# Strassen's scheme for the first product of the second MLP, last two batches

## The chip, the cores and the metric

The kernel runs on one core of a Trainium2 chip. The metric is the time on the device of one execution, in microseconds (us). The engines are named as in the profile: PE multiplies matrices (PEld is its loading of the stationary operand), DVE, ACT and POOL work on rows of 128 partitions, and SP issues the transfers (DMA).

## What is computed

Attention over 4 batches, 12 heads, 448 positions and head size 64, with normalised queries and keys, feeds two MLPs without a residual. Only the second one is changed.

```python
    x = attn_out.transpose(0, 2, 1, 3).reshape(B * S, H * D)      # 1792 x 768
    a = x @ w1; b = x @ w2; h = a * b @ w3; x = h @ w_out         # first MLP, 1024 wide
    h = x @ w_in                                                  # second MLP, 768 x 2048
    g = h * np.clip(h + 3.0, 0.0, 6.0) / 6.0
    return g @ w_out                                              # 2048 x 768
```

Inputs are float64 on the host and come as 64-bit words; the kernel converts them to float32 itself.

## The kernel before

Every product is made in float32 from halves: a value is split into a high part, rounded by ACT to the matmul's format, and a low part, the rest; `mm3` takes three matmuls for a product, high by high, high by low and low by high. A matmul has a stationary tile of 128 x 128 and 448 columns.

A scheduler sets the order of each engine's instructions, by the order in which the program issues them and by its own estimate of when each can run; `tc.issue_after` holds an instruction behind another one. Attention is first, with the product of w3 and w_out beside it, and the batches of the first MLP follow each other (`layer1`, `layer2`), the last one (batch 3) after the end of attention. Its weights `ws` are read back from DRAM, two halves of 768 columns in one transfer of 768 KB each, on SP's queue. In this time the weights of the second MLP begin to be read (`wr`, 768 KB of 64-bit words per tile of 128 x 768) and converted: `convert` takes two ACT and two DVE instructions per tile (L137, L138, L140, L143), and the results `wf`, 32 tiles, stay in SBUF to the end. `NA = 17` of them are made before the second MLP, the other 15 during its first batch.

The second MLP takes the batches in the order 3, 0, 1, 2, and in each 16 steps `m` of 128 hidden units. Step m has 18 matmuls for h (6 tiles of x, `mm3` each, into one bank), and 18 matmuls of the step before for the output (`l4_part`, six banks that collect over all m). Between them h becomes g: ACT makes the clipped part (L930), DVE multiplies by h (L931), ACT and DVE split the result (L934, L935). Each step splits its two weight tiles anew, ACT the high part (L851), POOL the low part (L852):

```python
    def split(q, tag, pool=None):
        t = (pool or lp).tile([P, 2, DM], F32R, tag=tag, bufs=2 if pool is None else 1, name=tag)
        nc.scalar.activation(t[:, 0, :], wf[q], AF.Copy)
        nc.gpsimd.tensor_sub(t[:, 1, :], wf[q], t[:, 0, :])
        return t
```

At the change of batch x is read from DRAM (`x2d`) and split by L826 and L827. Conversions of batch 3 stand in program order at the head of each step.

Of the kernel before, what the change touches and what calls it, by code (L numbers as in the profile page):

```python
# [47 lines left out]
def fused_kernel(ctx: ExitStack, tc: tile.TileContext, nat, qT, kT, vin, gq, gk,  # L48
# [8 lines left out]
    x2d = dpool.tile([B - 1, KD, P, S], F32, name="x2d")  # L57
    wpd = dpool.tile([KD * M1 // 6, P, 6, 2 * P], F32, name="wpd")
# [246 lines left out]
    def xsplit(i):  # L305
        d = L["pool"].tile([P, 2, S], F32R, tag="xhl", bufs=XB, name="xhl")
# [517 lines left out]
    def splitx2(n, src):
        d = x2p.tile([P, 2, S], F32R, tag="x2h", bufs=KD, name="x2h")
        nc.scalar.activation(d[:, 0, :], src, AF.Copy)  # L826
        nc.vector.tensor_sub(d[:, 1, :], src, d[:, 0, :])  # L827
        xh[n] = d

    L["x2"] = lambda n, ps: splitx2(n, ps[:, :S])  # L830

    def load_w(q):
        if q < 2 * M2:
            pool, tag, n = (wap, "wr", 2)
            if q >= NA + 2 and (q - NA) % 4 > 1:
                pool, tag, n = (lp, "wr", 1) if (q - NA) % 4 == 2 else (wap, "w0", 1)
            wr[q] = fetch(pool, (win, wo2)[q % 2][q // 2], DM, tag, bufs=n)

    def conv_w(q):
        r = wr.pop(q)  # L840
        wf[q] = wpools[-1].tile([P, DM], F32, name=f"wf{q}")
        if r.dtype == F32:
            nc.gpsimd.tensor_copy(wf[q], r)
        else:
            for _ in convert(wf[q].bitcast(I32), r):
                pass
        load_w(q + (2 if q < NA else 4))

    def split(q, tag, pool=None):
        t = (pool or lp).tile([P, 2, DM], F32R, tag=tag, bufs=2 if pool is None else 1, name=tag)  # L850
        nc.scalar.activation(t[:, 0, :], wf[q], AF.Copy)  # L851
        nc.gpsimd.tensor_sub(t[:, 1, :], wf[q], t[:, 0, :])  # L852
        return t

    load_w(0)
    load_w(1)
    step, q = 0, 0
    while not state["done"] or any(k >= now[0] for k in tasks):
# [3 lines left out]
        step += 1  # L862
# [75 lines left out]
    for e in (before, pend):  # L938
        for n in range(KD):
            with tc.issue_after(mm.ins) if mm else ExitStack():  # L940
                mm = l4_part(n, *e)
            if e is pend:
                out(n, t, acc)
# [47 lines left out]
```

## Time and profile before

| | |
|---|---|
| runs | 1225.72, 1224.61, 1220.15 us |
| median | 1224.61 us |
| profiled execution, first to last instruction | 1219.5 us |
| PE busy | 1160.4 us (95%), 5868 matmuls |
| DVE / ACT / POOL busy | 756.6 / 726.6 / 464.9 us |
| DMA | 203.73 MB, mean 167 GB/s |

The span is the time from the first to the last instruction of one execution that was profiled; the runs were timed apart and contain what lies around the span. Busy times are sums of the durations of an engine's instructions. In a window of the trace a matmul's duration overlaps that of the next, so PE's time per matmul is the window over its count and not the mean duration.

### The profile page before, as it was taken

The page shows a single profiled execution, that of the slowest core. Times are in us where ns is not written, and L with a number is a line of the kernel's source. Part 1 is how long each engine was busy: PE and PEld are TensorE (multiplying, and loading weights), DVE is VectorE, ACT ScalarE, POOL GpSimd, SP SyncE. Part 2 cuts the span into 40 slices and gives each one's busy share as a digit, 9 for nine tenths or more (in the row PEclk, how much of TensorE's full clock was granted, in tenths as well). Part 3 has the DMA queues.
Part 4 walks back from the last instruction along what each step waited for, and adds up shares of the span by engine and source line. Part 5 has one row for each costly group of instructions (what it writes and reads, how often), then busy time and mean ns, then how long its engine had stood idle before and what let it go on. Part 6 is the DMA issues. An engine that isn't in the chain of part 4 may idle for free.

```text
span 1219.5 us, 16961 instructions
## 1 busy us (share of the span) xinstructions
PE 1160.4 (95%) x5868; PEld 1020.5 (84%) x5868; DVE 756.6 (62%) x1474; ACT 726.6 (60%) x1401; POOL 464.9 (38%) x316
## 2 busy tenths in 40 slices
PE   3699998899999999999999999999999999999998
PEld 2457887777788999899999998999999999999997
DVE  6977888899976787677633447884333433343332
ACT  6888788899866767666634436664433443344332
POOL 3534224645522213212020005555455445544452
PEclk9799998999999999999999999999999999999999
DMA  7668565788987677666459985430200020001001
GB/s 277 209 220 239 191 188 196 251 284 293 334 265 254 222 224 249 228 240 197 148 187 360 355 304 207 156 101 23 91 1 1 4 88 1 1 1 46 1 1 46
DMA packets 64694, 203.73 MB, mean 167 GB/s; under 512 B 8544, under 2 KB 25440, under 8 KB 64608
## 3 DMA queue, kind: packets, MB, share of 16 engines
q1 hardware_dynamic: 64608, 202.65, 49.4%
q8 instruction: 46, 0.75, 0.3%
q14 instruction: 40, 0.33, 0.1%
HBM read 173.93 MB, written 28.68 MB: 166 GB/s over the span
## 4 chain that ended last, share of the span: by engine, by line
PE 75%; DVE 7%; ACT 5%; DMA 5%; issue 4%; POOL 3%; SPq 0%; ACTq 0%; POOLq 0%; DVEq 0%
PE bank L340 10%; PE acc L81 7%; PE acc L83 7%; PE acc L82 6%; PE h L81 6%; PE h L82 6%; PE h L83 6%; PE bank L345 5%; PE bank L592 4%; PE bank L81 3%; PE bank L82 3%; PE bank L83 3%; DVE PP L573 2%; PE bank L566 2%; PE bank L567 2%
## 5 line engine op out<-in xcount | busy, mean ns | idle before, releaser
L852 POOL TENSOR_TENSOR wis<-wf,wis 128x768 fp32r<-128x768 f32 x63 | 120.0, 1904 | 220.0 <-ACT wis L851 219.9
L340 PE MATMUL bank<-xhl,ws 128*128 128x448 f32 x768 | 184.9, 372 | 2.5 <-ACT bs L316 2.4
L931 DVE SCALAR_TENSOR_TENSOR u<-u,h 128x448 f32<-128x448 f32 x64 | 39.5, 618 | 210.6 <-ACT u L930 210.6
L340 PEld LDWEIGHTS bank<-xhl,ws 128*128 128x128 f32 x768 | 145.1, 191 | 16.5 <-ACT bs L316 3.1
L852 POOL TENSOR_TENSOR wos<-wf,wos 128x768 fp32r<-128x768 f32 x64 | 121.4, 1896 | 91.0 <-ACT wos L851 91.0
L585 ACT ACTIVATE PP<-PP,mx 112x448 f32<-112x448 f32 x192 | 127.2, 664 | 45.0 <-DVE mx L580 36.4
L573 DVE CUSTOM_DVE_ANT_0 PP<-bank,rb,rq 112x448 f32<-112x448 f32 x192 | 129.0, 675 | 34.8 <-PE bank L567 23.9
L83 PE MATMUL acc<-g,wos 128*128 128x448 f32 x384 | 141.3, 368 | 0.0
L82 PE MATMUL acc<-g,wos 128*128 128x448 f32 x384 | 141.3, 368 | 0.0
L81 PE MATMUL acc<-g,wos 128*128 128x448 f32 x384 | 140.0, 368 | 0.0
L81 PE MATMUL h<-x2h,wis 128*128 128x448 f32 x378 | 139.2, 368 | 0.5 <-DVE u L931 0.4
L82 PE MATMUL h<-x2h,wis 128*128 128x448 f32 x378 | 138.9, 367 | 0.0
L83 PE MATMUL h<-x2h,wis 128*128 128x448 f32 x378 | 137.4, 364 | 1.3 <-POOL wis L852 1.3
L930 ACT ACTIVATE u<-h,half 128x448 f32<-128x448 f32 x64 | 40.7, 636 | 156.0 <-PE h L83 156.0
L935 DVE TENSOR_TENSOR g<-u,g 128x448 fp32r<-128x448 f32 x64 | 105.2, 1645 | 37.5 <-ACT g L934 37.5
L851 ACT ACTIVATE wos<-wf 128x768 fp32r<-128x768 f32 x64 | 54.2, 847 | 85.9 <-PE acc L83 85.7
L601 ACT ACTIVATE xh<-bank 128x448 fp32r<-128x448 f32 (+1 forms) x156 | 83.0, 539 | 32.6 <-PE bank L592 29.4
L566 PE MATMUL bank<-K,Q 128*112 128x448 f32 x192 | 76.7, 400 | 25.6 <-DVE mx L573 13.1
L611 DVE TENSOR_TENSOR xl<-bank,xh 128x448 fp32r<-128x448 f32 x142 | 87.3, 616 | 21.9 <-ACT xh L601 20.6
L592 PE MATMUL bank<-ident,PP 112*128 112x112 f32 x672 | 94.4, 264 | 6.0 <-DVE xl L611 5.2
L592 PEld LDWEIGHTS bank<-ident,PP 112*128 112x128 f32 x672 | 77.7, 142 | 26.8 <-issue 6.8
L345 PE MATMUL bank<-xhl,ws 128*128 128x448 f32 x384 | 95.4, 367 | 0.0
(134 smaller groups left out, 2604.5 us busy)
## 6 DMA issues: line engine op xcount, KB each, us to landing
ws<-w12d SPq DMA_DIRECT2D x48, 768.0 KB
ws<-wpd SPq DMA_DIRECT2D x32, 768.0 KB
raw<-in_w_dram SPq DMA_DIRECT2D x32, 384.0 KB
w12d<-ws SPq DMA_DIRECT2D x16, 768.0 KB
wr<-in_wo_dram SPq DMA_DIRECT2D x16, 768.0 KB
qr<-in_qT_dram SPq DMA_DIRECT2D x24, 448.0 KB
kr<-in_kT_dram SPq DMA_DIRECT2D x24, 448.0 KB
nat<-in_nat_dram SPq DMA_DIRECT2D x23, 448.0 KB
```

Source lines behind the costliest of these rows:

```text
L81: nc.tensor.matmul(ps, lh, rh, start=first, stop=False)
L82: nc.tensor.matmul(ps, lh, rl, start=False, stop=False)
L83: return nc.tensor.matmul(ps, ll, rh, start=False, stop=last)
L340: nc.tensor.matmul(ps[:, :S], w[:, 0, ks], x[:, y, :], start=k == 0 and y == 0, stop=False)
L345: nc.tensor.matmul(ps[:, :S], w[:, 1, ks], L["xhl"][i][:, 0, :], start=False, stop=k == KD - 1)
L566: nc.tensor.matmul(ps[:CP, :S], qs, k1[:, j, :], start=True, stop=False)
L573: anchors[8 * i + s].append(nc.vector.tensor_tensor_reduce(out=T["PP", i][:, c, sl], in0=ps[:CP, :S], in1=T["rb", i][:, sl], op0=ALU.mult, ...
L585: anchors[8 * i + s].append(nc.scalar.activation(v, v, AF.Exp, bias=T["m", i][:, 8 + s : 9 + s], accum_out=T["sum", i][:, s : s + 1]))
L592: nc.tensor.transpose(ps[:, c * CP : c * CP + CP], src[:, c, kb * P : kb * P + P], ident[:CP, :CP])
L611: nc.vector.tensor_sub(lo, ps, hi)
L852: nc.gpsimd.tensor_sub(t[:, 1, :], wf[q], t[:, 0, :])
L935: nc.vector.tensor_sub(g[:, 1, :], u, g[:, 0, :])]
```

## The change

The second MLP is now made in three passes. Pass 0 is batch 3, pass 1 is batch 0, both with the same 18 and 18 matmuls per step. Pass 2 takes batches 1 and 2 together: for two steps of m (a pair j) and the two halves of the 768 inputs, the 2 x 2 block product of the weights with x of the two batches is made from seven products P1 to P7 of 9 matmuls each, in place of eight. The sums of weight blocks (S1 to S4) are made on DVE at each pair (L992), the sums of x (T1 to T4) once, on DVE; two banks, sA and sB, collect the products, ACT copies a bank (L1109), and DVE adds a copy to a bank (L1117). The output of batch 1 is made during the pass, that of batch 2 after it, from the stored `G`. Weights are split in halves of 384 columns (`wt`, seven tiles, six made ahead), by ACT and POOL in passes 0 and 1, and by ACT and DVE or POOL in turn in pass 2 (`halves`). The converted tiles don't stay: a ring of 11 tiles holds them, six more lie in tiles that pass 2 needs later for x, and each tile is written to DRAM (`wfd`) after use in its first pass and read again in the next two. Conversions are spread by `spend`, a budget in us per step. Lines move by one from the top (L83 is now L84, the transfers' L89 is L90, L140 is L141, L143 is L144), from L340 on by six.

```diff
+    wfd = dpool.tile([2 * M2, P, DM], F32, name="wfd")
...
+            if b == B - 1:
+                L["xm"].__exit__(None, None, None)
+                L["half"] = True
...
+    NWF, NWT, AHEAD2 = 11, 7, 6
+    BATCHES = {0: (B - 1,), 1: (0,), 2: (1, 2)}
...
+    for p in range(2):
+        for m in range(M2):
+            v = use("in", m)
+            items += [("I", p, m, v, h) for h in range(2)] + late
+            late = last_out(p, m) if m < M2 - 1 else []
+        late = last_out(p, M2 - 1)
+    items[1:3] = items[2:0:-1]
+    for j in range(M2 // 2):
+        v = (use("in", 2 * j), use("in", 2 * j + 1))
+        ls = late
+        if j:
+            ls = last_out(2, 2 * j - 2) + last_out(2, 2 * j - 1)
+        late = []
+        ls = [ls[: len(ls) // 2], ls[len(ls) // 2 :]]
+        for z in ("P1", "P2", "P6", 0, "P5", "P7", 1, "P3", "P4"):
+            items += ls[z] if z in (0, 1) else [(z, 2, j, v, z == "P4")]
+    for q in (M2 - 2, M2 - 1):
+        items += last_out(2, q)
+    for q in range(M2):
+        v = use("out", q)
+        items += [("M", 2, q, v, h) for h in range(2)]
...
+    def units():
+        for v, (kind, q) in enumerate(uses):
+            if v in extra:
+                while "left" not in xo:
+                    yield None
+                t = xtile(("11", "21", "T2")[(v - NWF) // 3], (v - NWF) % 3)
+                t = t.bitcast(F32).rearrange("p t s -> p (t s)")[:, :DM]
+            else:
+                z = ring.index(v) - NWF
+                while z >= 0 and ring[z] not in dropped:
+                    yield None
+                t = mp.tile([P, DM], F32, tag="wf", bufs=NWF, name="wf")
+            if v in fresh:
+                r = wr.pop(v)
+                if r.dtype == F32:
+                    nc.gpsimd.tensor_copy(t, r)
+                    yield 0.9
+                else:
+                    yield from convert(t.bitcast(I32), r)
+                load_raw()
+                yield 0.0
+            else:
+                dma(t, wfd[q + (M2 if kind == "out" else 0)])
+                yield 0.0
+            wf[v] = t
...
+    def drop(v):
+        kind, q = uses[v]
+        t = wf.pop(v)
+        dropped.add(v)
+        if v in fresh:
+            dma(wfd[q + (M2 if kind == "out" else 0)], t)
...
+    def halves(t, src, eng=None):
+        nc.scalar.activation(t[:, 0, :], src, AF.Copy)
+        if eng is None:
+            nsplit[0] += 1
+            eng = nc.vector if nsplit[0] % 2 else nc.gpsimd
+        eng.tensor_sub(t[:, 1, :], src, t[:, 0, :])
         return t
...
+    def xrest():
+        x = []
+        for k in range(KD // 2):
+            x.append(ptile())
+            dma(x[k], x2d[BATCHES[2][1], k + 3])
+        for k in range(KD // 2):
+            xo["22", k] = halves(xtile("22", k), x[k])
+            yield 1.2
+            d = ptile()
+            nc.vector.tensor_sub(d, xo["21", k][:, 0, :], xo["T2", k][:, 0, :])
+            nc.vector.tensor_sub(x[k], xo["21", k][:, 1, :], xo["T2", k][:, 1, :])
+            nc.vector.tensor_add(d, d, x[k])
+            xo["T4", k] = halves(xtile("T4", k), d)
+            yield 1.8
+
+    RIGHT = {"P1": "11", "P2": "21", "P6": "T2", "P5": "T1", "P7": "T3", "P3": "22", "P4": "T4"}
+    wt, sx = {}, {}
+
+    def prepare(i):
+        kind, p, j, v, h = items[i]
+        if kind[0] != "P":
+            upto(v)
+            t = mp.tile([P, 2, NH], F32R, tag="wt", bufs=NWT, name="wt")
+            wt[i] = halves(t, wf[v][:, h * NH : h * NH + NH], nc.gpsimd if p < 2 else None)
+            if h:
+                drop(v)
+            return
+        upto(v[1])
+        a11, a12 = wf[v[0]][:, :NH], wf[v[0]][:, NH:]
+        a21, a22 = wf[v[1]][:, :NH], wf[v[1]][:, NH:]
+
+        def temp(z, x, y, op):
+            sx[z] = xo["right"].tile([P, NH], F32, tag="sx", bufs=3, name="sx")
+            nc.vector.tensor_tensor(out=sx[z], in0=x, in1=y, op=op)
+            return sx[z]
+
+        if kind == "P6":
+            temp("S1", a21, a22, ALU.add)
+            temp("S2", sx["S1"], a11, ALU.subtract)
+        src = dict(P1=a11, P2=a12, P4=a22).get(kind)
+        if src is None:
+            if kind == "P7":
+                src = temp("S3", a11, a21, ALU.subtract)
+            elif kind == "P3":
+                src = temp("S4", a12, sx["S2"], ALU.subtract)
+            else:
+                src = sx["S2" if kind == "P6" else "S1"]
+        t = mp.tile([P, 2, NH], F32R, tag="wt", bufs=NWT, name="wt")
+        wt[i] = halves(t, src)
+        if h:
+            drop(v[0])
+            drop(v[1])
...
-        if step > 2 and q < NA and step % 3 == 0:
-            conv_w(q)
-            q += 1
-            if q == 1:
-                wnext = split(0, "w0", wap)
...
+        if L["cur"] < B * NU - 4 and (now[0] % 2 or "half" in L):
+            spend(1.5)
+        if "half" in L:
+            if "left" not in xo:
+                xo["left"] = d1.enter_context(tc.tile_pool(name="xl", bufs=1, side="left", **RW))
+            prep_to(ready[0] + 1 if ready[0] < AHEAD2 else 0)
...
+    def product(kind, i, ps, first):
+        w = wt.pop(i)
+        z = RIGHT[kind]
+        for k in range(KD // 2):
+            ks = slice(k * P, k * P + P)
+            x = xo[z, k]
+            for n, (a, c) in enumerate(((0, 0), (0, 1), (1, 0))):
+                mm = nc.tensor.matmul(ps[:, :S], w[:, a, ks], x[:, c, :], start=first and k == 0 and n == 0,
+                                      stop=k == KD // 2 - 1 and n == 2, skip_group_check=not first)
+        return mm
+
+    def strassen(i):
+        kind, p, j, _, _ = items[i]
+        if not swap:
+            swap.append((bank("s", "sA"), bank("s", "sB")))
+        a, c = swap[0]
+        own = c if kind in ("P2", "P5", "P3") else a
+        snap["mm"] = product(kind, i, own, kind in ("P1", "P2", "P5"))
+        r = own[:, :S]
+        if kind in ("P1", "P6", "P5"):
+            snap[kind] = utile()
+            nc.scalar.activation(snap[kind], r, AF.Copy)
+            return
+        if kind == "P4":
+            finish(p, j, 21, r)
+            swap[0] = (c, a)
+            return
+        s, z = {"P2": ("P1", 11), "P7": ("P5", 22), "P3": ("P6", 12)}[kind]
+        s = snap.pop(s)
+        nc.vector.tensor_add(s, r, s)
+        finish(p, j, z, s)
...
+    prep_to(AHEAD2)
+    xg = iter(())
+    for i, it in enumerate(items):
...
+        if i > 4:
+            with ExitStack() as es:
+                for z in done:
+                    es.enter_context(tc.issue_after(z.ins))
+                spend(1.0)
+        (plain if kind == "I" else strassen if kind[0] == "P" else layer4)(i)
```

SP's queue in the last batch of the first MLP, with `ws` the weights of the first MLP, `wr` the raw weights of the second, `wfd` the converted ones in DRAM. Before:

```order
L89 DMA ws<-w12d 128x1536 x2
L89 DMA wr<-in_win_dram 128x1536
L89 DMA ws<-w12d 128x1536 x2
L89 DMA wr<-in_wo_dram 128x1536
L89 DMA ws<-w12d 128x1536 x2
L89 DMA wr<-in_win_dram 128x1536
L89 DMA ws<-w12d 128x1536
L89 DMA wr<-in_wo_dram 128x1536
```

After the change:

```order
L90 DMA ws<-w12d 128x1536 x2
L90 DMA wr<-in_win_dram 128x1536
L90 DMA ws<-w12d 128x1536
L90 DMA wfd<-wf 128x768
L90 DMA ws<-w12d 128x1536
L90 DMA wr<-in_wo_dram 128x1536
L90 DMA ws<-w12d 128x1536
L90 DMA wfd<-wf 128x768
L90 DMA ws<-w12d 128x1536
L90 DMA wr<-in_win_dram 128x1536
L90 DMA ws<-w12d 128x1536
L90 DMA wfd<-wf 128x768
```

Each conversion is followed by a write of the converted tile, which stands between the loads of ws.

DVE's queue in the third and fourth step of batch 3 (L140/L141 and L143/L144 are the two DVE steps of a conversion, L931/L1048 the product with h, L935/L1056 the low half of g). Before:

```order
L931 SCALAR_TENSOR_TENSOR u<-u,h_8100 128x448
L935 TENSOR_TENSOR g<-u,g 128x448
L140 SCALAR_TENSOR_TENSOR wr<-wr 128x768
L143 SCALAR_TENSOR_TENSOR wf_8143<-wr 128x768
L931 SCALAR_TENSOR_TENSOR u<-u,h_8156 128x448
L935 TENSOR_TENSOR g<-u,g 128x448
L140 SCALAR_TENSOR_TENSOR wr<-wr 128x768
L143 SCALAR_TENSOR_TENSOR wf_8199<-wr 128x768
```

After the change:

```order
L1048 SCALAR_TENSOR_TENSOR u<-u,h_8093 128x448
L1056 TENSOR_TENSOR g<-u,g 128x448
L141 SCALAR_TENSOR_TENSOR wr<-wr 128x768 x2
L144 SCALAR_TENSOR_TENSOR wf<-wr 128x768 x2
L141 SCALAR_TENSOR_TENSOR wr<-wr 128x768
L144 SCALAR_TENSOR_TENSOR wf<-wr 128x768
L1048 SCALAR_TENSOR_TENSOR u<-u,h_8170 128x448
L1056 TENSOR_TENSOR g<-u,g 128x448
L141 SCALAR_TENSOR_TENSOR wr<-wr 128x768
L144 SCALAR_TENSOR_TENSOR wf<-wr 128x768
L141 SCALAR_TENSOR_TENSOR wr<-wr 128x768
```

Where one conversion stood between two products with h, two or three stand now.

DVE's queue at the change from batch 0 to the next (L827 and L928 make low halves, L969 and L970 combine parts of x, `wt` and `sx` are weights). Before:

```order
L931 SCALAR_TENSOR_TENSOR u<-u,h_9539 128x448
L935 TENSOR_TENSOR g<-u,g 128x448
L827 TENSOR_TENSOR x2h<-wr,x2h 128x448 x3
L827 TENSOR_TENSOR x2h<-w_8941,x2h 128x448 x3
L931 SCALAR_TENSOR_TENSOR u<-u,h_9588 128x448
L935 TENSOR_TENSOR g<-u,g 128x448
L931 SCALAR_TENSOR_TENSOR u<-u,h_9655 128x448
```

After the change:

```order
L1048 SCALAR_TENSOR_TENSOR u<-u,h_9920 128x448
L1056 TENSOR_TENSOR g<-u,g 128x448
L928 TENSOR_TENSOR wt<-wf,wt 128x384
L928 TENSOR_TENSOR xo<-xp,xo 128x448 x2
L969 TENSOR_TENSOR xp<-xo 128x448 x2
L928 TENSOR_TENSOR xo<-xp,xo 128x448
L970 TENSOR_TENSOR xp<-xp 128x448 x2
L969 TENSOR_TENSOR xp<-xo 128x448
L1048 SCALAR_TENSOR_TENSOR u<-u,h_9979 128x448
L928 TENSOR_TENSOR wt<-sx,wt 128x384
L970 TENSOR_TENSOR xp<-xp 128x448
L992 TENSOR_TENSOR sx<-wf,sx 128x384
```

Six subtractions of x stood behind the low half of g; now splits of weights and x, and sums of x, stand ahead of the last product with h of pass 1.

## Rows read from the trace of the kernel before

**Rows 1.** The page's first lines, and its chain that ended last

```profile
span 1219.5 us, 16961 instructions
PE 1160.4 (95%) x5868; PEld 1020.5 (84%) x5868; DVE 756.6 (62%) x1474; ACT 726.6 (60%) x1401; POOL 464.9 (38%) x316
...
PE 75%; DVE 7%; ACT 5%; DMA 5%; issue 4%; POOL 3%; SPq 0%; ACTq 0%; POOLq 0%; DVEq 0%
```

**Rows 2.** Windows: busy us (instructions) of each engine, granted clock, DMA share, GB/s

```profile
740.00:743.00 3.00, 2.89 (x16) 2.32 (x14) 1.85 (x3) 2.92 (x5) 0.00 (x0) 1.00 0.39 101
743.00:748.00 5.00, 4.16 (x19) 3.50 (x20) 3.90 (x3) 4.26 (x6) 4.98 (x3) 1.00 1.01 407
748.00:760.00 12.00, 11.14 (x55) 9.66 (x53) 11.90 (x10) 7.70 (x11) 10.27 (x5) 1.00 0.51 177
760.00:1200.00 440.00, 440.00 (x2142) 401.71 (x2141) 192.78 (x172) 195.82 (x289) 223.78 (x120) 1.00 0.11 36
```

**Rows 3.** Waits of PE from 560 to 760 us: total us, times, longest

```profile
PE h L83 <- POOL wis L852: 1.3, 2, 0.8
PE h L81 <- DVE u L931: 0.4, 1, 0.4
```

**Rows 4.** Windows ahead of the second MLP, with DMA share and GB/s last

```profile
640.00:660.00 20.00, 20.00 (x101) 18.54 (x100) 6.01 (x5) 7.54 (x12) 3.12 (x3) 1.00 0.93 345
660.00:680.00 20.00, 20.00 (x100) 18.54 (x99) 9.63 (x13) 8.89 (x14) 0.00 (x0) 1.00 0.98 382
680.00:700.00 20.00, 20.00 (x100) 18.53 (x99) 9.95 (x13) 8.36 (x13) 0.00 (x0) 1.00 0.95 354
700.00:720.00 20.00, 20.00 (x101) 18.52 (x100) 8.24 (x11) 7.18 (x11) 0.00 (x0) 1.00 0.90 324
```

**Rows 5.** Windows, the first 65 us of the second MLP

```profile
743.00:808.00 65.00, 63.30 (x305) 57.01 (x306) 56.92 (x44) 43.74 (x61) 42.94 (x20) 1.00 0.51 178
```

**Rows 6.** Groups by line, 743 to 808 us: count | busy us, mean ns

```profile
L143 DVE SCALAR_TENSOR_TENSOR wf<-wr 128x768 int32<-128x768 int32 x10 | 20.9, 2093 | 0.3
L935 DVE TENSOR_TENSOR g<-u,g 128x448 fp32r<-128x448 f32 x9 | 12.9, 1444 | 3.9 <-ACT g L934 3.9
L140 DVE SCALAR_TENSOR_TENSOR wr<-wr 128x768 int32<-128x768 int32 x9 | 10.7, 1191 | 2.8 <-ACT wr L138 2.8
L930 ACT ACTIVATE u<-h,half 128x448 f32<-128x448 f32 x9 | 5.7, 636 | 10.2 <-PE h L83 10.2
L931 DVE SCALAR_TENSOR_TENSOR u<-u,h 128x448 f32<-128x448 f32 x9 | 5.5, 611 | 1.0 <-ACT u L930 1.0
```

**Rows 7.** Timeline about 680 us: start, duration, engine, instruction, idle before

```profile
680.96 0.33 SPq L89 DMA_DIRECT2D wr<-in_wo_dram  x1
...
687.82 0.89 ACT L137 ACTIVATE wr<-wr 128x768 f32<-128x768 f32 x1 [2.54 <-DMA wr<-in_wo_dram]
```

**Rows 8.** Timeline of DVE and POOL, 743 to 757 us

```profile
743.02 1.83 POOL L852 TENSOR_TENSOR wis<-wf,wis 128x768 fp32r<-128x768 f32 x1 [87.51 <-ACT wis L851]
743.22 2.45 DVE L143 SCALAR_TENSOR_TENSOR wf<-wr 128x768 int32<-128x768 int32 x1
744.81 2.57 POOL L852 TENSOR_TENSOR wos<-wf,wos 128x768 fp32r<-128x768 f32 x1
747.34 2.55 POOL L852 TENSOR_TENSOR wis<-wf,wis 128x768 fp32r<-128x768 f32 x1
748.12 0.61 DVE L931 SCALAR_TENSOR_TENSOR u<-u,h 128x448 f32<-128x448 f32 x1
756.09 0.96 DVE L143 SCALAR_TENSOR_TENSOR wf<-wr 128x768 int32<-128x768 int32 x1
```

**Rows 9.** Groups of POOL by line over the span

```profile
L205 POOL TENSOR_TENSOR ws<-raw,ws 128x384 fp32r<-128x384 f32 x4 | 4.1, 1028 | 5.0 <-ACT ws L203 5.0
```

**Rows 10.** Groups by line, 808 us to the end

```profile
L827 DVE TENSOR_TENSOR x2h<-wr,x2h 128x448 fp32r<-128x448 f32 x12 | 9.2, 827 | 2.6 <-ACT x2h L826 2.6
L887 ACT ACTIVATE wr<-acc 128x448 f32<-128x448 f32 x9 | 4.9, 543 | 4.6 <-PE acc L83 4.6
```

More of the change, by code (lines that the diff above doesn't have):

```diff
@@ L824, in splitx2 @@
[L824 to L852, printed above, removed]
-        return t
@@ L855, in fused_kernel, with use, last_out @@
-    load_w(0)
-    load_w(1)
-    step, q = 0, 0
+    mp = d1.enter_context(tc.tile_pool(name="m2", bufs=1, side="left", **RW))
+    wf, wr, xo = {}, {}, {}
+    items, uses, late = [], [], []
+    def use(kind, q):
+        uses.append((kind, q))
+        return len(uses) - 1
+    def last_out(p, q):
+        v = use("out", q)
+        return [("L", p, q, v, h) for h in range(2)]
+    for p in range(2):
[4 more added lines that the diff above has]
+        late = last_out(p, M2 - 1)
@@ new lines, in fused_kernel @@
+    items[1:3] = items[2:0:-1]
[11 more added lines that the diff above has]
+    for q in range(M2):
+        v = use("out", q)
+        items += [("M", 2, q, v, h) for h in range(2)]
@@ new lines, in fused_kernel, with load_raw @@
+    fresh = []
+    for v, x in enumerate(uses):
+        if x not in [uses[z] for z in fresh]:
+            fresh.append(v)
+    dropped = set()
+    extra = range(NWF, NWF + 6)
+    ring = [v for v in range(len(uses)) if v not in extra]
+    raws = [0, None]
+    def load_raw():
+        n = raws[0]
+        if n < len(fresh):
+            raws[0] += 1
+            kind, q = uses[fresh[n]]
+            if "right" in xo and raws[1] is None:
+                raws[1] = n
+            pool = mp if raws[1] is None or (n - raws[1]) % 4 > 1 else xo["right"]
+            wr[fresh[n]] = fetch(pool, (win if kind == "in" else wo2)[q], DM, "wr")
@@ new lines, in fused_kernel, with nonlinear, gsplit @@
+    load_raw()
+    load_raw()
+    def nonlinear(src, out):
+        u = utile()
+        nc.scalar.activation(u, src, AF.Relu, bias=half, scale=1.0 / 6.0)
+        return nc.vector.scalar_tensor_tensor(out=u if out is None else out, in0=u, scalar=1.0, in1=src,
+                                              op0=ALU.min, op1=ALU.mult), u
+    G, g, done = {}, {}, []
+    def gsplit(p, b, q, src):
+        t = xo["right"].tile([P, 2, S], F32R, tag="g", bufs=4, name="g")
+        done[:] = [nc.scalar.activation(t[:, 0, :], src, AF.Copy),
+                   nc.vector.tensor_sub(t[:, 1, :], src, t[:, 0, :])]
+        g[p, b, q] = t
@@ L884, in out @@
+    acc = {}
+    def out(n, t):
+        o = utile()
         if n % 2:
@@ L937, in fused_kernel, with layer4 @@
-    mm = None
[L938 to L943, printed above, removed]
+    def layer4(i):
+        kind, p, q, _, h = items[i]
+        b = int(kind == "M")
+        w = wt.pop(i)
+        x = g[p, b, q] if h == 0 else g.pop((p, b, q))
+        for n in range(3 * h, 3 * h + 3):
+            if q == 0:
+                acc[n] = bank(TAGS[1 + n // 2], "acc")
+            ns = slice(n % 3 * P, n % 3 * P + P)
+            with tc.issue_after(snap["mm"].ins) if (p, q) == (2, M2 - 2) and not b else ExitStack():
+                mm3(acc[n][:, :S], w[:, 0, ns], w[:, 1, ns], x[:, 0, :], x[:, 1, :], q == 0, q == M2 - 1)
+            if q == M2 - 1:
+                out(n, BATCHES[p][b])
```

187 lines of the change are left out of this document (111 added, 76 removed).

## The prediction

> **What bounds the kernel now.** I read the page first: the reader is to see that the tensor engine (PE) is busy 95% of the span, and that 75% of the chain that ended last is PE [rows 1]. Then the windows of the second MLP, since the change starts there: from 760 to 1200 us PE is busy 440.00 of 440.00 us at granted clock 1.00, which is 2142 matmuls, so one costs 440.00 / 2142 = 0.2054 us; DVE is busy 192.78, ACT 195.82, POOL 223.78 us of it, and DMA a share of 0.11 [rows 2]. No other engine can hold PE up there. Then the waits of PE ahead of it: they are 1.3 us on POOL and 0.4 us on DVE, at the entry into this MLP [rows 3]. So whatever leaves PE's instruction count shortens the span at 0.2054 us apiece, as long as what is put on the other engines stays under PE. Of the stages that the change loads, two are full now: the DMA before the MLP (share 0.90 to 0.98 between 640 and 720 us [rows 4]) and DVE in batch 3, which is busy 56.92 of 65 us from 743 to 808 us [rows 5].
>
> **What the change removes.** Batches 1 and 2 cost 2 x 16 x 18 = 576 matmuls in their first product. The scheme takes 8 pairs x 7 products x 9 = 504. PE's list has 72 matmuls fewer and nothing else new: 72 x 0.2054 = **-14.8 us**, if PE stays dense.
>
> **Entry into the MLP.** Now only the first split is made ahead and PE waits for the next ones: over the three windows from 740 to 760 us it is busy 2.89 + 4.16 + 11.14 = 18.19 of 20 us [rows 2], a loss of 1.8 us. After the change six halves are ready before the MLP starts, so these waits go. But the third bank of h is asked for two matmuls after the end of the first, and that bank frees only when relu and product are done: 0.636 + 0.611 us [rows 6] plus 0.2 us of handing over, against 2 x 0.2054: a wait of 1.0 us. Net **-1 us** (from -1.8, if nothing waits, to +1, if a split is late as now too).
>
> **DMA before the MLP.** Each weight tile that is converted there is now also written: 0.39 MB behind each 0.79 MB read, on SP's queue between loads of ws. By rows, four windows from 640 us moved 345, 382, 354 and 324 GB/s, mean 351 [rows 4]; a write per 7.3 us adds 54, making 405, above the 382 that a window at share 0.98 reached. Over 80 us that leaves the queue about 5 us behind. In the list a load of ws stands 73 matmuls (15 us) before its first use; a load at this density took from its issue at 680.96 to its use at 687.82 us, 7 us [rows 7]. So 7 + 5 is still under 15: I take **+0.5 us** (from 0 to 5). Queued behind these loads on SP are only the next raw weights, which ACT waits for (2.54 us here [rows 7]), not PE.
>
> **Batch 3 (pass 0): the dense stretch.** Before, 12 weight tiles are converted on DVE in 315 matmuls of this stretch, after, 15 in 257 (52.8 us), since fewer were done ahead. The rows show how DVE and POOL get on: the POOL split 743.02 to 744.85 us and the DVE conversion 743.22 to 745.67 overlap in the trace, yet DVE needs another 0.82 us after POOL has ended, about what it takes alone (0.96); the next POOL split, begun at 744.81, takes 2.57 us instead of the 1.83 of the first, and ends 1.71 after DVE does [rows 8]. So the two take turns. Where DVE reads PSUM (the product with h) it ran in 0.61 us under a POOL split [rows 8]. The price of a turn is then 0.82 us for a conversion step, 0.47 for a subtraction of 448 columns (0.61, as the product, less the same 0.14), and for a POOL split of 384 columns between 0.86 (half of 1.71) and 1.03, the nearest row of that width [rows 9]; I take 0.95, as both ends are near. After the change the stretch holds 30 conversion steps, 9 subtractions and 28 splits: 24.6 + 4.2 + 26.6 = 55.4 us. The 7 products with h cost DVE 4.3 us more, half of it under POOL: 57.6 us against 52.8 of PE. About 2 us of it are taken up by what is prepared ahead, so **+3 us** (from 0, with splits of 0.86 and all products hidden, 52.9 us, to 11.7: a conversion step at the measured mean of the two lines, (2093 + 1191) / 2 = 1.64 us, a subtraction at 1.44 and a product at 0.61 [rows 6] make 66.5 us on DVE, less 52.8 and the 2 in hand). Before, the same count gave 25 x 0.82 + 9 x 0.47 + 20 x 1.71 = 59 us in a window of 65 [rows 5, 6], and PE waited only at its start, so the sum is a fair guide. What is late first is g's low half behind conversions, then PE at layer 4; the list already lets PE take first-product matmuls there.
>
> The Trainium skill states the same lock ("SBUF — State Buffer", section "SBUF: two separate sides"): a DVE operation with two SBUF inputs and a GpSimd operation that reads SBUF exclude each other for a whole instruction. By it the stretch is the sum of both engines, as these rows have it; by adding only DVE's own 33 us it would fit easily, and the 3 us would be 0.
>
> **Switch to batches 1 and 2.** In place of 6 subtractions of x (0.827 us each [rows 10]), DVE has nine SBUF operations in a row within 27 matmuls (5.5 us), and the product with h that frees a bank for P2 stands behind them: nine at 0.61 and four POOL splits at 0.95 make 9.3 us against 32 matmuls, 6.6: 2.7 us late; some start early, so **+2 us** (from 0 to 5).
>
> **The 7 products.** Each pair adds snapshots (ACT reads a bank, nearest row 0.543 us [rows 10]), additions with a bank on DVE (as the product, 0.61), weight sums and the splits. Over the pass's 735 matmuls (151 us) DVE has 54 operations with a bank or with h at 0.61, 14 subtractions of g at 0.61, and 66 of 384 columns at 0.53 (0.61 scaled from 448): 76 us; POOL has 42 splits at 0.95, 40; ACT 153 operations of 0.45 to 0.64, some 80. DVE and POOL taking turns at all of it make 116 of 151. Light. What can wait is a bank reused after 9 to 13 matmuls (1.85 to 2.7 us) against chains of 0.7 (a snapshot) to 1.5 us (relu and product); one blocked DVE operation ahead makes 3.1 and 1.2 us late. I take one such wait in the pass and small ones: **+1.5 us** (from 0 to 8, one in nearly every pair).
>
> **Weights through DRAM.** Passes 1 and 2 read 0.39 MB per 3.7 us, 107 GB/s, where the share is 0.11 now [rows 2]: 0. If this cover were gone, PE would wait 3 us or so for each late tile. The last copies and stores keep their order: 0.
>
> **Sum.** -14.8 - 1 + 0.5 + 3 + 2 + 1.5 = -8.8 us. Made against the profiled execution (span 1219.5 us) that is 1210.7; the runs shown have their median at 1224.61, 5.1 above the span, and the lowest at 1220.15. Added to the median: **1215.8, said as 1216 us**.
>
> **Rivals.**
> (a) PE stays dense: all new waits are hidden and only -14.8 - 1 counts: 1209. For it: DVE is busy only 192.78 of 440 us [rows 2]. Against: DVE was at 56.92 of 65 us in batch 3 and gets more conversions. Chance 0.16.
> (b) Turns and switches eat the gain: the dense stretch at 11.7 us: -8.8 + 8.7 = -0.1, 1224.5. For it: the group means, in which a 0.96 us step lasts 2.09 [rows 6, 8]. Chance 0.21.
> (c) Slower: DVE's line in the dense stretch becomes the bound, every conversion step at the blocked 2.05 us: 30 x 2.05 + 9 x 1.44 + 4.3 = 78.8 us against 52.8 + 2: 24 us of waits, in all -8.8 + 21 = +12, 1237. It decides above 18 us of waits there, a mean step near 1.85 us. For it: L143 alone averages 2.09. Against: L140 averages 1.19 [rows 6], and half as long POOL splits block half as long. Chance 0.11.
> (d) Transfers: if the DMA can hold no more than 354 GB/s (one of the rows), the queue before the MLP is 12 us behind, of which 8 are reserve, and the dense stretch's 339 GB/s leaves nothing to catch up: +4 us of late raw weights and as much of late conversions: -8.8 + 8 = -0.8, 1223.8. For it: share 0.93 to 0.98 now. Against: the window with 382 GB/s, and 407 from 743 to 748 us [rows 2, 4]. Chance 0.10. The Trainium skill ("DMA: Bandwidth & Descriptors", section "Specifications") gives about 358 GB/s as a core's limit to HBM, which is rival (d); the rows go past that figure here, so they hold against it.
>
> **Chances.** The forecast has 0.42. Some 0.5% (6.1 us) is what a measurement of this kernel tells from no change. Faster by more: 0.16 of (a) and 0.37 of the forecast's 0.42, with 0.02 of (b): 0.55. Within: the rest of the forecast, most of (b) and (d): 0.32. Slower: (c) and 0.02 of (d): 0.13. Range: 1209 (a) to 1228, which leaves out most of (c) and the far end of (a).
>
> **What would show it.** Right: 72 matmuls fewer at an unchanged 0.2054 us in batch 0 and in the last phase; PE waits of some 3 us in all in batch 3, put down to DVE or POOL; 2 us where P2 starts; scattered waits in the 7 products; no PE wait on DMA. Wrong, if PE in batch 3 is busy under 0.85 of its time (b, c), if ACT waits for raw weights many us at a stretch (d), or if each pair shows a wait of over 1 us, for which the terms here would be too small.

## The result, and the profile after

The changed kernel took 1211.19 us in the median of 4 runs (1209.86 to 1213.16), the kernel before 1223.13 us (1220.15 to 1225.72): a ratio of 0.9904, with a 95% interval from 0.9881 to 0.9926, which is 11.7 us (9 to 14.6). The forecast was 8.8 us and 1216.

The first lines of the page of the changed kernel answer to [rows 1]:

```profile
span 1209.2 us, 17549 instructions
PE 1145.1 (95%) x5796; PEld 1005.0 (83%) x5796; DVE 798.2 (66%) x1604; ACT 756.6 (63%) x1554; POOL 461.4 (38%) x389
```

The 72 matmuls are gone, and PE's share of the span is what it was. The windows of batch 3 come next (us, then busy time and count of PE, PEld, DVE, ACT and POOL, the granted clock, DMA share and GB/s):

```profile
735.00:750.00 15.00, 14.03 (x69) 12.61 (x68) 6.03 (x9) 6.71 (x13) 1.82 (x3) 1.00 0.73 254
780.00:800.00 20.00, 18.24 (x87) 15.61 (x86) 18.94 (x17) 16.70 (x29) 16.41 (x11) 1.00 0.96 337
800.00:820.00 20.00, 19.17 (x93) 16.89 (x92) 18.52 (x17) 14.35 (x27) 18.30 (x13) 1.00 0.80 276
820.00:840.00 20.00, 18.95 (x93) 16.82 (x92) 10.41 (x11) 11.83 (x23) 15.70 (x14) 1.00 0.50 159
```

PE is idle for 0.97 us in the first of these, not at all from 750 to 780 us, and for 1.76 + 0.83 + 1.05 = 3.6 us from 780 to 840 us, where DVE is busy 18.94 and 18.52 of 20 us. A window ahead of this stretch, and one behind it:

```profile
660.00:680.00 20.00, 20.00 (x101) 18.53 (x100) 9.37 (x12) 11.22 (x19) 6.69 (x6) 1.00 1.02 418
840.00:1160.00 320.00, 319.62 (x1559) 292.03 (x1558) 169.85 (x238) 162.96 (x320) 146.61 (x133) 1.00 0.36 113
```

Ahead of the MLP the transfers reached 418 GB/s and PE lost nothing; from 840 to 1160 us it is dense but for 0.38 us, in the pass with the seven products too.

Idle time is not all that a wait costs, so the same matmuls are also compared by their count. Matmul 3683 of the program starts at 766.35 us before and at 765.37 us after, matmul 4143 at 860.90 and 865.16 us; none of the 72 that are gone lies ahead of them. The windows between these starts hold most of batch 3, before and after (their counts also take in what overlaps an end):

```profile
766.35:860.90 94.55, 94.55 (x462) 86.32 (x460) 64.35 (x53) 53.33 (x77) 51.42 (x27) 1.00 0.24 81
765.37:865.16 99.79, 96.15 (x462) 85.54 (x460) 64.71 (x58) 62.14 (x111) 74.92 (x56) 1.00 0.66 226
```

The same 460 matmuls take 5.2 us longer, though PE counts as idle for only 3.6 us of it; the last section says why.

The waits of PE from 690 us to the end (total, times, longest):

```profile
PE h L82 <- DVE u L1048: 2.5, 3, 1.0
PE acc L83 <- DVE g L1056: 2.2, 4, 0.9
PE sB L1095 <- DVE u L1117: 0.2, 1, 0.2
```

All are put down to DVE. They name the two places of the forecast, the entry (one wait of 1.0 us) and batch 3; 0.4 us lie about the start of the pass with seven products, half of it on g and half on sB. The groups of DVE and POOL from 760 to 840 us (count, busy us and mean ns) answer to [rows 6] and [rows 9]:

```profile
L928 POOL TENSOR_TENSOR wt<-wf,wt 128x384 fp32r<-128x384 f32 x31 | 41.7, 1372 | 7.4 <-ACT wt L924 7.3
L141 DVE SCALAR_TENSOR_TENSOR wr<-wr 128x768 int32<-128x768 int32 x16 | 23.0, 1442 | 1.4 <-ACT wr L139 1.4
L1056 DVE TENSOR_TENSOR g<-u,g 128x448 fp32r<-128x448 f32 x10 | 11.3, 1130 | 4.5 <-ACT g L1055 4.5
L1048 DVE SCALAR_TENSOR_TENSOR u<-u,h 128x448 f32<-128x448 f32 x10 | 6.1, 611 | 5.8 <-ACT u L1047 5.8
```

A conversion step, 0.96 us alone [rows 8], takes 1.44 us, and a split of 384 columns 1.37; the product with h, which reads PSUM, stays at 0.61. One of the waits in order of time, from the timeline (start, duration, engine, instruction):

```profile
788.97 6.79 POOL L928 TENSOR_TENSOR wt<-xo,wt 128x384 fp32r<-128x384 f32 x4 [1.40 <-ACT wt L924]
790.79 0.62 ACT L1047 ACTIVATE u<-h,half 128x448 f32<-128x448 f32 x1
791.42 1.77 DVE L141 SCALAR_TENSOR_TENSOR wr<-wr 128x768 int32<-128x768 int32 x1
793.11 0.61 DVE L1048 SCALAR_TENSOR_TENSOR u<-u,h 128x448 f32<-128x448 f32 x1
793.65 1.24 DVE L144 SCALAR_TENSOR_TENSOR wf<-wr 128x768 int32<-128x768 int32 x1
793.76 0.58 ACT L1055 ACTIVATE g<-u 128x448 fp32r<-128x448 f32 x1 [1.51 <-DVE u L1048]
794.81 1.44 DVE L1056 TENSOR_TENSOR g<-u,g 128x448 fp32r<-128x448 f32 x1
796.31 0.47 PE L83 MATMUL acc<-g,wt 128*128 128x448 f32 x1 [0.80 <-DVE g L1056]
```

POOL runs four splits end to end, 6.79 us or 1.70 each, which is one turn of each engine: 0.82 for a conversion step and 0.88 for a split of 1.02 us, less the same 0.14. ACT has its part ready at 791.41 (L1047), but the conversion step L141 shares its time with the splits and ends at 793.19, so the product with h starts 1.7 us late. Then the next conversion step and the low half of g share theirs too, and PE gets g's low half 0.80 us late.

### The profile page after: what moved, and what is told of

It is laid out like the page before. It is cut to its first block, busy times and chain, and to the rows that moved or that the text cites. A ratio compares the mean times of both kernels' runs of the same rounds, so it can differ in the third digit from the quotient of the medians.

```text
span 1209.2 us, 17549 instructions
## 1 busy us (share of the span) xinstructions
PE 1145.1 (95%) x5796; PEld 1005.0 (83%) x5796; DVE 798.2 (66%) x1604; ACT 756.6 (63%) x1554; POOL 461.4 (38%) x389
## 5 line engine op out<-in xcount | busy, mean ns | idle before, releaser
L928 POOL TENSOR_TENSOR wt<-wf,wt 128x384 fp32r<-128x384 f32 x160 | 181.7, 1147 | 264.1 <-ACT wt L924 226.6
L924 ACT ACTIVATE wt<-wf 128x384 fp32r<-128x384 f32 x204 | 103.8, 520 | 94.0 <-PE acc L84 47.4
L346 PEld LDWEIGHTS bank<-xhl,ws 128*128 128x128 f32 x768 | 144.2, 190 | 15.8 <-ACT bs L322 2.3
L83 PE MATMUL acc<-g,wt 128*128 128x448 f32 x384 | 141.9, 370 | 2.3 <-DVE g L1056 2.2
L84 PE MATMUL acc<-g,wt 128*128 128x448 f32 x384 | 137.9, 367 | 0.0
L82 PE MATMUL acc<-g,wt 128*128 128x448 f32 x384 | 134.5, 368 | 0.0
L561 POOL TENSOR_TENSOR vo<-vr,vo 128x512 fp32r<-128x512 f32 x22 | 29.8, 1356 | 137.9 <-ACT vo L560 127.2
L83 PEld LDWEIGHTS acc<-g,wt 128*128 128x128 f32 x384 | 72.1, 188 | 11.7 <-DVE g L1056 5.1
L553 POOL TENSOR_TENSOR K<-kr,K 128x448 fp32r<-128x448 f32 x48 | 58.5, 1240 | 50.8 <-ACT K L551 50.8
L82 PEld LDWEIGHTS acc<-g,wt 128*128 128x128 f32 x384 | 71.9, 188 | 7.3 <-ACT g L1055 0.5
L84 PEld LDWEIGHTS acc<-g,wt 128*128 128x128 f32 x384 | 72.1, 188 | 6.7
L351 PEld LDWEIGHTS bank<-xhl,ws 128*128 128x128 f32 x384 | 71.9, 188 | 6.5 <-issue 0.2
L675 POOL TENSOR_TENSOR xs<-xs,rsb 128x448 f32<-128x448 f32 x24 | 29.4, 1226 | 119.1 <-DMA rsb<-rsd 70.7
```

The source lines that it names most:

```text
L82: nc.tensor.matmul(ps, lh, rh, start=first, stop=False)
L83: nc.tensor.matmul(ps, lh, rl, start=False, stop=False)
L84: return nc.tensor.matmul(ps, ll, rh, start=False, stop=last)
L346: nc.tensor.matmul(ps[:, :S], w[:, 0, ks], x[:, y, :], start=k == 0 and y == 0, stop=False)
L351: nc.tensor.matmul(ps[:, :S], w[:, 1, ks], L["xhl"][i][:, 0, :], start=False, stop=k == KD - 1)
L924: nc.scalar.activation(t[:, 0, :], src, AF.Copy)
```

## The experiments

**The seven products taken out.** Batches 1 and 2 follow one after the other with the plain first product, and their low halves of weights all go to POOL. The 16 tiles of w_in are read from DRAM once more.

```diff
-    BATCHES = {0: (B - 1,), 1: (0,), 2: (1, 2)}
+    BATCHES = {0: (B - 1,), 1: (0,), 2: (1,), 3: (2,)}
-    for p in range(2):
+    for p in range(4):
...
-    for j in range(M2 // 2):
-        v = (use("in", 2 * j), use("in", 2 * j + 1))
...
+    items += late
```

> Edit: batches 1 and 2 are taken one after the other with the plain first product (18 matmuls per step), everything else as in the changed kernel: weights through DRAM, halves of 384 columns, the same batch 3. Theory 'count': the gain over the kernel before is the 72 matmuls, 14.8 us, less about 3 us of waits in batch 3 and at the switch; with the 72 back the kernel is 14.4 to 15.2 us longer than the changed one (1211.2), so 1224.5 to 1228, 1.002 to 1.004 of the kernel before. PE waits: 3 to 5 us in batch 3 and at the entry, none after it. Rival 'scheme': passing the weights through DRAM, or the lighter splits, give part of the gain themselves; then this kernel is faster than the one before by 3 us or more.

It took 1228.29 us, 1.0047 of the kernel before (1.0031 to 1.0062). From the last matmul of the first MLP to the last of all its profiled execution has 1219.47 - 743.12 = 476.35 us, the changed kernel 1205.14 - 743.92 = 461.22, which is 15.1 us less. Of this 0.7 us lies in batch 0, where both do the same work (matmuls 4143 to 4700 take 115.11 us here, 114.44 in the changed kernel). From matmul 4700 on it is 240.00 - 225.54 = 14.5 us, where 14.8 was worked out for the 72 matmuls. PE's waits from 690 us on:

```profile
PE h L82 <- DVE u L1035: 2.5, 3, 1.0
PE acc L83 <- DVE g L1043: 2.0, 3, 0.9
```

They are the same two groups. So 'count' holds and 'scheme' falls: the passing through DRAM gives nothing by itself, and without the products the change would have cost some 6 us (3.8 to 7.6). That is just over the expected 1224.5 to 1228. In its profile batch 3's 460 matmuls take 99.72 us, 5.2 more than before, where the expectation went by some 3 us of waits; the rest of the miss is not resolved.

**No writes to DRAM.** The output is another one, since batches 0, 1 and 2 read other weights of the same size.

```diff
-                dma(t, wfd[q + (M2 if kind == "out" else 0)])
+                z = q + (M2 if kind == "out" else 0)
+                dma(t, w12d[z % M1, z // M1 % 2][:, z // 16 * DM : z // 16 * DM + DM])
-        if v in fresh:
-            dma(wfd[q + (M2 if kind == "out" else 0)], t)
```

> Edit: the converted weights are not written to DRAM; batches 0, 1 and 2 read tiles of the same size from another buffer in DRAM (weights of the first MLP) in their place, so the output is another one; batch 3 is as before. It takes 12.6 MB of transfers out, most of them before and in batch 3. Theory 'turns': the 3.6 us that PE waits in batch 3 come from DVE and POOL taking turns; they stay at 3 to 4.5 us, DVE stays busy over 18 of 20 us from 780 to 820. Rival 'transfers': raw weights come late for conversion because of the writes; the waits in batch 3 fall under 1 us and the time by 3 us.

It took 1212.54 us, 0.9918 (0.9903 to 0.9933). Windows from 780 us, and the one with the 460 matmuls:

```profile
780.00:800.00 20.00, 19.06 (x89) 15.96 (x88) 16.84 (x16) 17.37 (x28) 10.74 (x9) 1.00 0.67 229
800.00:820.00 20.00, 18.73 (x91) 16.47 (x90) 18.53 (x17) 15.08 (x29) 16.68 (x12) 1.00 0.55 183
768.54:868.60 100.06, 96.59 (x461) 85.54 (x460) 63.62 (x58) 62.22 (x111) 70.63 (x56) 1.00 0.48 155
```

The DMA share is down from 0.96 to 0.67 and from 0.80 to 0.55, yet PE is idle for 100.06 - 96.59 = 3.5 us, and the 460 matmuls take 100.06 us for 99.79, as with the writes. 'Transfers' falls; the expectation of DVE over 18 held in one of the two windows.

**No low halves in batch 3.** Every step of it reads one and the same low half, so the output is another one.

```diff
+            if p:
+                wt[i] = halves(t, s, nc.gpsimd if p < 2 else None)
+            else:
+                nc.scalar.activation(t[:, 0, :], s, AF.Copy)
+                if "low" not in xo:
+                    xo["low"] = mp.tile([P, NH], F32R, name="low")
+                    nc.gpsimd.tensor_sub(xo["low"], s, t[:, 0, :])
+                wt[i] = t
...
+        lo = w[:, 1, :] if p else xo["low"]
```

> Edit: in batch 3 the low halves of the weights are not made by POOL; every step reads one and the same low half, made once, so the output is another one. POOL is idle in batch 3 but for three splits of x; ACT, DVE and the transfers have the same work as in the changed kernel. Theory 'turns': a conversion step on DVE takes 0.96 us instead of 1.44, DVE is busy 13 of 20 us or less from 780 to 820, and PE's waits in batch 3 fall from 3.6 us to under 0.5; the entry's 1.0 us stays. Time 3 to 3.6 us less than the changed kernel. Rival 'transfers' (or ACT as the bound): the waits stay at 3 us or more, since neither has less to do.

It took 1204.95 us, 0.9854 (0.9837 to 0.9872). Windows, and the conversion step from 760 to 840 us:

```profile
780.00:800.00 20.00, 20.00 (x100) 18.38 (x99) 15.27 (x18) 17.10 (x30) 1.53 (x1) 1.00 1.02 394
762.94:857.02 94.08, 94.08 (x462) 86.43 (x460) 48.25 (x58) 62.46 (x111) 10.45 (x9) 1.00 0.66 237
```

```profile
L141 DVE SCALAR_TENSOR_TENSOR wr<-wr 128x768 int32<-128x768 int32 x15 | 15.3, 1021 | 7.4 <-ACT wr L139 7.2
```

With POOL nearly still, PE is dense although the transfers run at 394 GB/s and ACT is busy 17.10 of 20 us. DVE takes 1.02 us a step, though this window is fuller than expected (15.27 for 13): it holds 18 instructions for 17. That leaves the turns. The time fell by 6 us, where 3 to 3.6 were expected from the idle time; the 460 matmuls take 94.08 us for 99.79, so 5.7 of it lies in batch 3.

**A slower pace of conversions.** The same work, spread over more steps.

```diff
-                spend(1.0)
+                spend(0.6)
```

> Edit: the budget per half step for conversions is 0.6 us in place of 1.0, so the conversions of batch 3 are spread over nearly all of its 16 steps: about 1.3 per step in place of 2 to 2.5 in its first part; the work is the same. Theory 'turns': the conversions' density is what makes DVE the bound, PE's waits in batch 3 fall from 3.6 us to 0 to 1.5; the time is 2 to 3.5 us under the changed kernel, 1208 to 1209. Rival: the waits come back at the end of batch 3, where the tiles left over are then forced at two per step, 3 us or more in all, and the time stays.

It took 1207.02 us, 0.9880 (0.9857 to 0.9902). PE was dense from 750 to 820 us, and then waited for the tile that was left over (and 0.4 us on POOL just behind it):

```profile
PE h L82 <- ACT wt L924: 1.6, 1, 1.6
```

Both sides of the expectation were right in part: density makes the waits, and what is put off too far is forced. The expected 1208 to 1209 was missed by 1 to 2 us. The interval overlaps that of the changed kernel (0.9881 to 0.9926), and in the profile batch 3's 460 matmuls take 98.11 us, only 1.7 less, so how much this pace gains by itself is not shown.

**A pace between the two.**

```diff
-                spend(1.0)
+                spend(0.75 if q % 2 else 0.6)
```

> Edit: the budget per half step for conversions alternates between 0.6 and 0.75 us by step, so a bit more than one and a half conversions per step, between the changed kernel and the slower pace, which left tiles over and had PE wait 2 us near 835 us. Theory 'turns': DVE is no longer full from 780 to 820 (under 17 of 20 us), nothing is forced at the end, PE waits under 1 us in batch 3 beside the entry's 1.0; the time is 3 to 4 us under the changed kernel, 1207 to 1208, no slower than the slower pace. Rival: any conversion that is put off costs PE a wait where it is forced; 2 us or more of waits remain.

It took 1206.51 us, 0.9874 (0.9858 to 0.9890), beside 1211.97 us, 0.9917 (0.9901 to 0.9933), of the changed kernel run again on the same chip: faster than both kernels, and just under the expected 1207 to 1208. Windows and waits:

```profile
780.00:800.00 20.00, 20.00 (x99) 18.40 (x98) 14.78 (x14) 16.04 (x27) 14.50 (x13) 1.00 0.77 269
765.69:860.77 95.08, 94.56 (x461) 86.28 (x460) 67.06 (x61) 64.74 (x115) 70.86 (x55) 1.00 0.71 238
```

```profile
PE acc L83 <- DVE g L1056: 0.5, 1, 0.5
```

DVE has room again (14.78 of 20 us) and of 3.6 us of idle PE 0.5 is left. Batch 3's 460 matmuls take 95.08 us for 99.70 in the changed kernel run again, 4.6 of the 5.5 us by which the medians differ.

**The changed kernel again.** No edit.

> No edit: the changed kernel again. Two things are asked. The waits of PE: 1.0 us at the entry and 3.6 us of idle PE in batch 3 if they belong to the program, other numbers if they belong to one execution. And the time from one matmul to the next in batch 0, for which the executions so far showed 0.2002, 0.2047 and 0.2067 us with the same instructions: if it belongs to the program it is 0.2047 again, if to the execution another of these. Time 1209.5 to 1213, ratio 0.988 to 0.992.

Time as above. The window with the 460 matmuls of batch 3:

```profile
768.01:867.71 99.70, 96.03 (x461) 85.49 (x460) 64.65 (x58) 62.01 (x111) 74.80 (x56) 1.00 0.67 226
```

PE is idle for 99.70 - 96.03 = 3.7 us, and the 460 matmuls take 99.70 us for 99.79: the waits belong to the program. The time from one matmul to the next in batch 0 was 0.2067 us and not 0.2047: the program alone doesn't set it. Whether the execution or the chip does is not shown.

**Low halves twice.** In batch 3 POOL makes each low half of the weights a second time.

```diff
+            s = wf[v][:, h * NH : h * NH + NH]
+            wt[i] = halves(t, s, nc.gpsimd if p < 2 else None)
+            if p == 0:
+                nc.gpsimd.tensor_sub(t[:, 1, :], s, t[:, 0, :])
```

> Edit: in batch 3 POOL makes each low half of the weights twice, with the same result. Theory 'turns': DVE is blocked by each of them; in the dense stretch 54 splits at 0.88 (1.02 alone less 0.14) and DVE's 29 us and 2 us of products make 78 us against 52.8, 24 us of waits; in all of batch 3 25 to 31 us, put down to DVE operations and POOL. A conversion step takes about 2 us. Rival 'POOL alone': the engines don't block each other and PE only waits when POOL itself is late: 79 splits at 1.02 are 80 us for 74 us of PE, under 9 us of waits, and conversion steps stay at 1.44 us or less.

It took 1244.99 us, 1.0190 (1.0168 to 1.0212). Waits of PE from 690 us, two windows (the second with the 460 matmuls), and groups from 760 to 840 us (L985 is the second split):

```profile
PE acc L84 <- POOL wt L985: 8.8, 8, 2.6
PE h L84 <- POOL wt L985: 8.5, 7, 3.6
```

```profile
780.00:800.00 20.00, 15.86 (x63) 12.76 (x62) 17.93 (x14) 12.72 (x20) 20.00 (x14) 0.88 0.89 303
766.41:897.00 130.59, 109.22 (x462) 89.11 (x461) 79.21 (x63) 63.88 (x114) 130.59 (x105) 0.93 0.54 176
```

```profile
L141 DVE SCALAR_TENSOR_TENSOR wr<-wr 128x768 int32<-128x768 int32 x15 | 25.2, 1685 | 4.9 <-ACT wr L139 4.9
L985 POOL TENSOR_TENSOR wt<-wf,wt 128x384 fp32r<-128x384 f32 x15 | 23.9, 1610 | 0.0
L928 POOL TENSOR_TENSOR wt<-wf,wt 128x384 fp32r<-128x384 f32 x16 | 21.8, 1378 | 0.0
```

From 750 to 960 us PE was idle 22.7 us, a little under the 25 to 31 of 'turns' and far over the 9 of 'POOL alone'. A split that takes 1.02 us alone takes 1.38 and 1.61, and a conversion step 1.69 (2 were expected). So both engines lengthen, and neither one's own time is the bound. But the one that is late is now POOL, busy for all of the 130.59 us, in 17.3 us of the waits, and not DVE. The Trainium skill ("SBUF — State Buffer", section "SBUF: two separate sides") describes a lock between a DVE operation with two SBUF inputs and a GpSimd operation that reads SBUF, which whichever starts first holds for its whole instruction; these rows, 1.69 us for 0.96 on DVE and 1.38 to 1.61 for 1.02 on POOL, agree with it. The time rose by 33 us, of which the 460 matmuls have 130.59 - 99.70 = 30.9; the last section says how they exceed the idle time.

**Low halves on POOL in the pass of seven products.** The edit is in `halves`, which also makes the low halves of x, so 14 of those move to POOL too, some of them in batch 3:

```diff
-            eng = nc.vector if nsplit[0] % 2 else nc.gpsimd
+            eng = nc.gpsimd
```

> Edit: in the pass with the seven products POOL makes all low halves of weights, 83 in place of 42, and DVE none. Theory 'light': DVE and POOL taking turns make 73 us of POOL and at most 54 us of DVE in 151 us, so the pass stays without PE waits over 1 us in all and the time within 1 us of the changed kernel. Rival: the pass has as little room as batch 3 had, since the additions with a bank are now queued behind blocked sums on DVE; then waits of 0.5 us or more appear in most pairs, 4 us or more in all.

It took 1213.35 us, 0.9931 (0.9907 to 0.9955), not to be told from the changed kernel run again. PE's waits from 900 us and two windows of the pass:

```profile
PE sB L1095 <- DVE u L1117: 1.4, 1, 1.4
```

```profile
985.00:1000.00 15.00, 13.57 (x65) 11.67 (x64) 11.53 (x15) 8.62 (x18) 12.59 (x11) 1.00 0.40 134
1010.00:1130.00 120.00, 120.00 (x589) 110.45 (x588) 52.71 (x76) 61.52 (x119) 66.89 (x66) 1.00 0.26 79
```

Inside the pass PE is dense with POOL at 66.89 and DVE at 52.71 of 120 us, so it has room. The only wait from 900 us on, 1.4 us on sB (0.2 in the changed kernel), is at its start, where the forecast had put 2 us; the expectation of under 1 us in all missed it. With two runs, the time can't show a difference of 1 us.

## Why the prediction was right

The sign, the range and the kind of each large term were right. The size came out near in part because errors cancel: batch 3 was dearer than forecast, and the switch and the seven products were nearly free. At 1211.19 us the result is in fact nearer to rival (a), 1209, than to the forecast of 1216, though (a)'s condition, no new waits, did not hold.

Counted by matmuls, from start to start, in the profiled executions (us):

| matmuls, in the program's order | before | changed | changed, again |
|---|---|---|---|
| 3000 to 3540, ahead of the MLP | 108.57 | 108.62 | 108.62 |
| 3540 to 3683, entry | 32.07 | 30.45 | 30.46 |
| 3683 to 4143, batch 3 | 94.55 | 99.79 | 99.70 |
| 4143 to 4700, batch 0 | 114.51 | 114.44 | 115.11 |
| 4700 to the last, batches 1 and 2 | 240.11 | 225.54 | 225.50 |

Beside the forecast, with the first two columns:

| term | forecast | measured |
|---|---|---|
| 72 matmuls, switch and seven products | -14.8 + 2 + 1.5 = -11.3 | -14.6 |
| entry | -1 | -1.6 |
| DMA before the MLP | +0.5 | 0 |
| batch 3 | +3 | +5.2 |
| batch 0 | 0 | -0.1 |
| sum | -8.8 | -11.0 |

The medians give 11.7 us (9 to 14.6). Some 1.5 us more of the way from 1216 to 1211.19 come from the median that the forecast was added to, 1224.61 of three runs, where four have 1223.13.

At the **entry** the wait of 1.0 us came as worked out: relu and product against two matmuls. The gain is 1.6 us and not 1, since the waits that went cost more than the 1.8 us for which PE was idle.

**Batch 3** is the term that was mis-sized most. The kind of wait was right: first the product with h, then g's low half stand behind conversion steps that POOL's splits lengthen. The size was not, and as far as it was it was luck. The forecast put its 3 us into 257 matmuls, up to 800 us; beside the middle pace 2.8 us were lost there by count (56.57 for 53.75), and 2.6 us more in the next 223 matmuls, where 11 further conversion steps of DVE begin. Nor are the 2.8 us what the sum counted. Up to 800 us the trace has 28 conversion steps, 7 subtractions and 26 splits, where 30, 9 and 28 were counted; at the forecast's own prices they make 53.1 us with the products, and with a split at 0.88 us 51.3, against 52.8 and the 2 in hand. So the sum over both engines would have given no wait at all. What it leaves out is the order in DVE's queue: a single step of 1.77 us ahead of the product is enough, as the rows above show.

That the waits come from the turns, and not from transfers or ACT, is shown by the runs that took away the writes (100.06 us for the 460 matmuls, waits stay), the low halves (94.08, waits go) and the density (95.08, waits nearly go). Rivals (b) and (c), which took the blocked means of before as prices, were too dear because POOL's operations are half as long now: a step took 1.44 us, for 1.64 and 2.05.

The other mis-sized terms are smaller. For the **switch** I let nine DVE operations and four splits stand between the last product with h and the bank of P2. In the trace P2 had its bank in time; PE waits 0.2 us on g before and 0.2 us on the next use of sB, behind L1117. For the **seven products** I charged one blocked addition; none was late, and even with all low halves on POOL there was none inside the pass. For the **DMA** I took 382 GB/s as about the most; 418 was reached, rival (d) falls with it, and without the writes the time did not fall.

Rival (a), a dense PE, missed by the 5.2 us of batch 3. It is what the middle pace nearly reaches.

## What to carry to other kernels

Where two engines exclude each other, add up the operations of both in the stretch that is dense, at their times alone, and compare with the bound engine's time there; the mean over a longer stage hides it. A sum near that time says that waits are likely; how long they are depends on what stands in the queue ahead of the operation that the bound engine waits for. To price a wait, compare the time of the same instructions by count, and not the idle time alone. Work that only has to be done by a due time should be spread at the rate at which it falls due: one number in the pace was worth 4.6 us of batch 3 here (5.5 in the medians), and too slow a pace brings a wait at the end. A scheme that saves work on the bound engine is worth its instruction count if its extra work lands in stages where the other engines are idle, as the pass of seven products shows.

## What the runs showed of the hardware

**A wait costs more than the idle time that the profile shows.** In the changed kernel 3.6 us of idle PE in batch 3 go with 5.2 us of loss, and the granted clock was 1.00 throughout. The rows of the run with the slower pace show the shape of a wait:

```profile
834.88 0.47 PE L82 MATMUL h<-xo,wt 128*128 128x448 f32 x1 [1.56 <-ACT wt L924]
835.19 0.37 PE L83 MATMUL h<-xo,wt 128*128 128x448 f32 x1
835.97 0.47 PE L84 MATMUL h<-xo,wt 128*128 128x448 f32 x1 [0.41 <-POOL wt L928]
836.27 0.36 PE L82 MATMUL h<-xo,wt 128*128 128x448 f32 x1
836.48 0.36 PE L83 MATMUL h<-xo,wt 128*128 128x448 f32 x1
...
837.82 0.57 PE L82 MATMUL h<-xo,wt 128*128 128x448 f32 x1
838.19 0.57 PE L83 MATMUL h<-xo,wt 128*128 128x448 f32 x1
```

A matmul's duration is 0.36 us and the next starts after 0.20, so PE counts as busy for 0.16 us after the next one should have begun; and behind a wait the first step is 0.30 us. That makes some 0.26 us beside the idle time of each wait; six waits make 1.6 us, which is the difference.

**Two waits close together were followed by a lower clock.** Further on in the same rows the step is 0.37 us, nine times from 837.09 to 840.43, and then 0.20 again:

```profile
837.10:840.50 3.40, 3.40 (x11) 3.01 (x10) 2.75 (x4) 2.49 (x4) 1.72 (x2) 0.50 0.83 336
```

The granted clock is 0.50 there, the engine's lower level (1.2 GHz, against 2.4). Nine times 0.17 us more make 1.5 us on top of 2.0 of waits. A single wait of 1.4 us did not do it: with all low halves on POOL, PE waited so long on sB, and the granted clock stayed at 1.00. How much waiting it takes is not shown. In the run with low halves twice it was 0.88 from 780 to 800 us; 37 steps of that run are at about 0.37 us, 6 of its 33 us. The rest of what batch 3 lost there is 19 us more of idle time and what goes with each wait.

**The same matmuls have several steps.** In batch 0, with the same instructions and PE never waiting, 70 us hold 11 matmuls more in the run without low halves (first row) than in the changed kernel run again (second):

```profile
900.00:970.00 70.00, 70.00 (x351) 65.58 (x350) 22.52 (x34) 34.34 (x67) 40.36 (x39) 1.00 0.33 102
900.00:970.00 70.00, 70.00 (x340) 63.61 (x339) 23.48 (x29) 31.74 (x62) 43.91 (x41) 1.00 0.40 118
```

From start to start the mean there is 0.2002 us in the one and 0.2067 in the other, 0.2055 before and 0.2047 in the first execution of the changed kernel. The step also changes within one execution: without low halves it is 0.2067 us from 860 to 900 us and 0.2000 behind that. Matmuls 4143 to 4700 took 112.85 to 112.90 us in three executions (no writes, no low halves, slower pace) and 114.44 to 115.15 in six others. What sets the step is open; it wasn't tried. The three short ones were all on one chip, where the run with the seven products taken out had a long one, so the chip isn't excluded. Nor do executions agree in the stage before: the last matmul of the first MLP lay at 743.92 us in one execution of the changed kernel and at 746.54 in the other. Differences of 2 to 3 us between two profiles are therefore no evidence by themselves; the same matmuls by count, in one stage and with a wait in the rows behind it, are.
